# Spectral and shifted-MLP layer in fp16 halves: another order of low halves, GpSimd's refinement chains and the first shifted tiles

## The chip, the core and the metric

The kernel runs on one core of a Trainium2 chip. The core has five engines with instruction streams of their own: TensorE (PE in the profile; its weight loads are listed as PEld), VectorE (DVE), ScalarE (ACT), GpSimd (POOL) and SyncE (SP), which here issues DMAs. In this program they wait for each other through semaphores. The metric is the device time of one execution in microseconds (us), lower is better.

## The reference

Input x is 2048 rows of 448 features. It is normalised by row, and the normalised xn goes into two branches, whose results are added to x:

```python
xn = layernorm(x)
A  = irfft2(rfft2(xn) * (w_r + 1j*w_i))
h  = gelu(layernorm(xn) @ w1)                 # 448 -> 448
hs = concat(four quarters of 112 features of h,
            moved by +1, -1, +2, -2 rows, zeros let in) @ w2
x1 = xn + hs
B  = x1 + gelu(layernorm(x1) @ w3) @ w4       # 448 -> 1792 -> 448
out = x + A + B
```

All of it is fp32.

## The kernel before

Products are made in fp16 on TensorE: each operand is split into a high half (the value rounded to fp16) and a low half (what is left), and a product is the sum of high by high, high by low and low by high. So weights and activations are both split by other engines ahead of TensorE, usually the high half by ScalarE (a copy) and the low half by VectorE (scaled value minus high half).

The rows are cut into 16 blocks of 128: block b holds rows b, b + 16, b + 32 and so on, so that a shift by one row is a shift by one block. Blocks are worked in four groups of four: group 0 is blocks 14, 15, 0, 1, group 1 is 2 to 5, group 2 is 6 to 9, group 3 is 10 to 13. A block within a group is a unit (i from 0 to 3). What happens to a group, with the names in the code:

- `norm1` (from L322): mean and variance by VectorE (`sta` L309, `mva` L310), then a chain of tiny operations: `va` (L333, L334), a first guess of the inverse root in integers, `vy` (L335, L336), `nma` (L338). With it each block is normalised in place, one by each of the engines in the list `apply` (L345 for ScalarE, L348 for GpSimd and VectorE). The guess is coarse. GpSimd refines it meanwhile (L356 to L364), and makes from it the factor `gsc` (L365) that the gelu applies, and the scales of the later residual (`cs`, `nm`, L369 to L376).
- `turn_pe` (L396) transposes the group's four blocks on TensorE, by feature chunk t (0 to 3), 4 transposes each, into PSUM. `turn_copy` takes the high half out on ScalarE (L406) and the low half on VectorE (L407): xT. Group 3 is turned by DMA instead.
- `w1_in` (L446) does the product with w1, 44 matmuls for a group: 12 for each of chunks 0 to 2 and 8 for the short chunk 3. In group 0 all four units go forward together by chunk and by pass (high by high, high by low, low by high), as w1 is being split at the time; in later groups one unit at a time.
- `w1_unit` (L458): gelu on ScalarE (L466), high half (L467), low half on VectorE (L468), then a DMA transpose issued by SyncE (L471) puts the result, h, back with features on the partitions.
- `w2_tile` (L475): for one block, 12 matmuls (L487): three for each of the four quarters k. Quarter 2 is read from block b - 2, 0 from b - 1, 1 from b + 1, 3 from b + 2. So tile 0 needs blocks 14 and 15 (units 0 and 1 of group 0), 1 (unit 3) and 2 (unit 0 of group 1); tile 1 needs blocks 15 and 0, 2 and 3. VectorE adds the result to the block (L489).

After that come the second layernorm (`ln2`), the product with w3 (L417), gelu and halves `hf` (L732, L734, L735), the product with w4 (L754), in the function `front` and what calls it, and the two Fourier transforms as matrix products, woven in by halves c: among them `px` (L649), taken out of PSUM by ScalarE (`te`, L654) and multiplied by VectorE (L655, L656), added by GpSimd (L658).

`split_w` (L268 to L287) splits a weight tile. With `high=P` GpSimd scales it, makes the high half (L275) and the low one (L276); with `low=P` GpSimd scales (L279), ScalarE makes the high half (L281), GpSimd the low one (L282); without, ScalarE does the high half (L284), VectorE the low one (L285). `powers` finds a power of two for a tensor's scale, through one small matmul (`pm`, L254) that sums over partitions.

The order on each engine is fixed when the kernel is built: a scheduler simulates the program and issues each engine's instructions in the order in which they become ready there. `behind(key)` holds instructions back in that order until those recorded in `after[key]` have been issued; it adds no wait at run time. What runs at run time is therefore the order and the data's own semaphores. The program uses eight banks of PSUM, four names (`mm`, `tr`, `sp`, `acc`) of two each, which are handed on from user to user.

The main sequence (L825 to L895) begins with group 0, and goes on:

```python
    with behind("p2"):
        T1(1)
...
    with behind("a1"):
        w1_unit(0, 0, first[0])
        n1.append(norm1(2, [P, V, A, P], 1))
    with behind("a1"), behind("n", 2):
        for k in range(1, 4):
            w1_unit(0, k, first[k])
```

`first` are the four PSUM banks in which group 0's w1 product is summed up; `T1(g)` is `turn_pe` and `turn_copy` for all four chunks; `("n", 2)` is group 2's `nma`.

## Time and profile before

| | us |
|---|---|
| median of 3 runs | 415.0 |
| lowest, highest | 414.98, 415.24 |
| profiled execution, its time | 415.5 |
| its span, first to last instruction | 413.7 |
| TensorE busy within the span | 406.3 |
| VectorE, ScalarE, GpSimd busy | 297.8, 247.7, 113.4 |

The profile is of one execution; its span and its time differ by what lies ahead of the first instruction and behind the last. In a row of the timeline the first number is the start in us, the second the length; then come engine, source line, operation, output <- inputs by the program's names, shape, and how many instructions the row stands for. A bracket at the end gives idle time of that engine just before it and what ended it. Rows of matmuls are pipelined: a row's length includes about 0.16 us in which its last matmul drains while the next row has begun.

### The profile page before, as it was taken

The page shows a single profiled execution, that of the slowest core. Times are in us where ns is not written, and L with a number is a line of the kernel's source. Part 1 is how long each engine was busy: PE and PEld are TensorE (multiplying, and loading weights), DVE is VectorE, ACT ScalarE, POOL GpSimd, SP SyncE. Part 2 cuts the span into 40 slices and gives each one's busy share as a digit, 9 for nine tenths or more (in the row PEclk, how much of TensorE's full clock was granted, in tenths as well). Part 3 has the DMA queues.
Part 4 walks back from the last instruction along what each step waited for, and adds up shares of the span by engine and source line. Part 5 has one row for each costly group of instructions (what it writes and reads, how often), then busy time and mean ns, then how long its engine had stood idle before and what let it go on. Part 6 is the DMA issues. An engine that isn't in the chain of part 4 may idle for free.

```text
span 413.7 us, 8526 instructions
## 1 busy us (share of the span) xinstructions
PE 406.3 (98%) x3310; PEld 289.7 (70%) x3310; DVE 297.8 (72%) x636; ACT 247.7 (60%) x427; POOL 113.4 (27%) x204
## 2 busy tenths in 40 slices
PE   7998999999999999999999999999999999999996
PEld 3555555765667777776788888787766776677885
DVE  5998999798843757863688889865877687667122
ACT  4688869973647866762578888864443334342321
POOL 2697620101136746400031121210212221221000
PEclk9999999999999999999999999999999999999999
DMA  8959779914921374447056665620000113224001
GB/s 285 329 202 171 148 150 336 161 61 89 203 68 44 91 238 164 113 79 174 14 131 172 154 155 142 154 69 3 2 0 2 68 37 121 90 68 133 24 0 46
DMA packets 53496, 48.53 MB, mean 117 GB/s; under 512 B 37600, under 2 KB 48480, under 8 KB 53456
## 3 DMA queue, kind: packets, MB, share of 16 engines
q1 hardware_dynamic: 53456, 47.99, 43.7%
q8 instruction: 26, 0.43, 0.4%
q14 instruction: 14, 0.11, 0.1%
HBM read 35.52 MB, written 3.67 MB: 95 GB/s over the span
## 4 chain that ended last, share of the span: by engine, by line
PE 91%; POOL 3%; DVE 3%; DMA 2%; issue 0%; ACT 0%; POOLq 0%
PE pw L417 33%; PE acc L754 31%; PE pw L487 9%; PE pw L446 4%; PE pu L677 3%; PE ps L575 3%; PE pe L697 2%; PE pp L632 2%; PE px L649 2%; PE py L719 2%; DVE sta L309 1%; DMA xt<-x 1%; DMA h<-hs 1%; DVE xT L407 1%; POOL w2p L276 0%; POOL xt L348 0%
## 5 line engine op out<-in xcount | busy, mean ns | idle before, releaser
L417 PE MATMUL pw<-x2mem,w3p 128*128 128x256 f16 x1232 | 149.0, 273 | 0.0
L754 PE MATMUL acc<-w4p,hf 128*128 128x448 f16 (+1 forms) x714 | 138.1, 341 | 0.0
L417 PEld LDWEIGHTS <-w3p 128*128 128x128 f16 x1232 | 118.6, 98 | 19.1
L754 PEld LDWEIGHTS <-hf 128*128 128x128 f16 x714 | 69.4, 98 | 48.3 <-DVE hf L735 0.3
L732 ACT ACTIVATE pw<-pw,pe 128x512 f32<-128x512 f32 x56 | 36.7, 656 | 64.0 <-PE pw L417 64.0
L735 DVE SCALAR_TENSOR_TENSOR hf<-pw,h,hf 128x512 f16<-128x512 f32 x56 | 41.8, 748 | 40.9 <-ACT hf L734 40.6
L487 PE MATMUL pw<-w2p,h 112*128 112x448 f16 x192 | 40.0, 352 | 1.1 <-DMA h<-hs 1.1
L734 ACT ACTIVATE hf<-pw,h 128x512 f16<-128x512 f32 x56 | 38.1, 684 | 1.1
L658 POOL TENSOR_TENSOR z<-te 128x450 f32<-128x450 f32 x16 | 16.3, 1017 | 74.0 <-DVE te L656 74.0
L446 PE MATMUL pw<-w1p,xT 128*128 128x448 f16 x176 | 35.5, 352 | 0.4 <-ACT xT L406 0.3
L704 POOL TENSOR_TENSOR e<-e 128x226 f32<-128x226 f32 x16 | 11.3, 709 | 77.5 <-ACT e L701 74.7
L487 PEld LDWEIGHTS <-h 112*128 112x128 f16 x192 | 18.5, 98 | 17.3 <-DMA h<-hs 1.6
L446 PEld LDWEIGHTS <-xT 128*128 128x128 f16 x176 | 17.0, 98 | 16.5 <-ACT xT L406 0.9
L639 ACT ACTIVATE pf<-pp 64x450 f16<-64x450 f32 x32 | 17.3, 541 | 16.6 <-DVE pf L640 8.1
L701 ACT ACTIVATE e<-pe 128x452 f32<-128x452 f32 x16 | 8.8, 548 | 26.6 <-PE pe L697 26.6
L640 DVE TENSOR_TENSOR pf<-pp,pf 64x450 f16<-64x450 f32 x32 | 19.9, 621 | 5.3 <-ACT pf L639 5.0
L555 POOL TENSOR_TENSOR xr<-xf 128x452 f32<-128x452 f32 x8 | 9.2, 1155 | 31.6 <-issue 25.4
L654 ACT ACTIVATE te<-px 64x450 f32<-64x450 f32 x32 | 17.2, 539 | 0.5
L712 DVE TENSOR_TENSOR vh<-e,vh 128x448 f16<-128x448 f32 x16 | 10.0, 625 | 9.7 <-ACT vh L711 9.7
L566 DVE TENSOR_TENSOR xh<-f,xh 128x452 f16<-128x452 f32 x16 | 11.8, 780 | 6.9 <-ACT xh L565 6.9
L558 POOL TENSOR_TENSOR f<-xr 128x452 f32<-128x452 f32 x16 | 16.1, 1030 | 0.6
L706 DVE TENSOR_TENSOR e<-e 128x113 f32<-128x113 f32 x16 | 9.5, 593 | 7.8 <-POOL e L704 7.8
(171 smaller groups left out, 600.0 us busy)
## 6 DMA issues: line engine op xcount, KB each, us to landing
wc<-wf SPq DMA_DIRECT2D x32, 225.0 KB, 3.7
wl<-wf SPq DMA_DIRECT2D x8, 450.0 KB, 3.8
xf<-x SPq DMA_DIRECT2D x8, 448.0 KB, 3.5
xt<-x SPq DMA_DIRECT2D x3, 896.0 KB, 13.0
w3raw<-w SPq DMA_DIRECT2D x3, 896.0 KB, 16.0
xr<-x SPq DMA_DIRECT2D x12, 224.0 KB, 2.6
out<-xr SPq DMA_DIRECT2D x12, 224.0 KB, 2.0
gn<-c_g SPq DMA_DIRECT2D x16, 128.0 KB, 3.3
```

Source lines behind the costliest of these rows:

```text
L417: T.matmul(ps_out, wp[:, wi + t, cols], xT[:, xi + t, tok], start=t == 0 and wi + xi == 0, stop=t == 3 and wi == 4)
L446: m = T.matmul(pm[:, :D], xTs[g][:, xi + t, 128 * i:128 * i + 128], w1p[:, wi + t], start=t == 0 and p == 0, stop=t == 3 and p == 2)
L487: T.matmul(pm[:, :D], hT[g][:112, 4 * hi + k, o:o + 128], w2p[:, wi, k], start=n == 0, stop=n == 11)
L558: P.tensor_tensor(out=f[:, :, k:k + 2].rearrange("p b s d -> p s b d"), in0=u[:, :, 0], in1=u[:, :, 1], op=op)
L639: A.activation(out=hi, in_=src, func=AF.Copy)
L640: V.tensor_tensor(out=lo, in0=src, in1=hi, op=ALU.subtract)
L654: A.activation(out=e[64 * h:64 * h + 64], in_=px_[64 - 64 * h:128 - 64 * h, :2 * DF], func=AF.Copy)
L658: P.tensor_tensor(out=z, in0=t[:, 0], in1=t[:, 1], op=ALU.add)
L732: A.activation(out=pm, in_=pm, func=AF.Gelu_apprx_tanh, scale=r3)
L734: i = A.activation(out=h[:, 0], in_=pm, func=AF.Copy, scale=h3)
L735: j = V.scalar_tensor_tensor(out=h[:, 1], in0=pm, scalar=h3, in1=h[:, 0], op0=ALU.mult, op1=ALU.subtract)
L754: m = T.matmul(to, h[:, hi, o:o + 128], w4p[0][:, wi, f, r], start=f == 0 and n == 0, stop=f == 13 and n == 2)
```

## The change

In words, with the lines of the kernel before:

1. `split_w`: the splitting on GpSimd (`high=P`) now leaves the low half to be placed by the caller. A new form, used for chunk 1 of w1: GpSimd scales the tile into a spare buffer, ScalarE makes the high half, and GpSimd the low half. Before, VectorE made that low half (L285).
2. `norm1`: the factor `gsc` becomes a function of its own (`gain`), apart from the refinement and the scales. For group 2, `va` stands behind the halves of unit 3 of group 0 (`behind(0, 3)`), and its blocks are normalised by GpSimd, VectorE, ScalarE, VectorE instead of GpSimd, VectorE, ScalarE, GpSimd.
3. GpSimd's order: refinement and gain of group 0, then refinement and gain of group 1, then w2's scaling, high and low halves; the scales of groups 0 to 2 all stand behind w2's last low half.
4. `w1_unit`: in group 0 the gelu of unit i stands behind the halves of unit i - 2.
5. TensorE's order: group 1's first eight transposes and the small matmul of `powers` for w2 go ahead of the last four matmuls of group 0's w1 product, the other eight behind. That small matmul gets a bank of its own. `w2_tile` is cut in two for tiles 0 and 1: quarters 2 and 0 of both (12 matmuls), then group 2's transposes, then quarters 1 and 3 (12), then group 2's w1 product.
6. w2's quarters 1 and 3: scaled by GpSimd earlier, high half by ScalarE behind group 0's last halves, low half by GpSimd behind group 2's normalisation.
7. In the transform: `te` records its instructions, and the halves `hf` of front 4, unit 1, stand behind `te` of half 12 (one unit's halves, L734 and L735).

```diff
--- before.py
+++ after.py
@@ -272,9 +272,13 @@
             return i.ins, lambda: V.scalar_tensor_tensor(out=lo, in0=src, scalar=s, in1=hi, op0=ALU.mult, op1=ALU.subtract).ins
         if high is P:
             P.tensor_scalar(out=src, in0=src, scalar1=s, scalar2=0.0, op0=ALU.mult, op1=ALU.add)
-            P.tensor_scalar(out=hi, in0=src, scalar1=1.0, scalar2=0.0, op0=ALU.mult, op1=ALU.add)
-            i = P.tensor_tensor(out=lo, in0=src, in1=hi, op=ALU.subtract)
-            return (i.ins,)
+            i = P.tensor_scalar(out=hi, in0=src, scalar1=1.0, scalar2=0.0, op0=ALU.mult, op1=ALU.add)
+            return i.ins, lambda: P.tensor_tensor(out=lo, in0=src, in1=hi, op=ALU.subtract)
+        if isinstance(low, bass.AP):
+            P.tensor_scalar(out=low, in0=src, scalar1=s, scalar2=0.0, op0=ALU.mult, op1=ALU.add)
+            i = A.activation(out=hi, in_=src, func=AF.Copy, scale=s)
+            j = P.tensor_tensor(out=lo, in0=low, in1=hi, op=ALU.subtract)
+            return i.ins, j.ins
         if low is P:
             i = P.tensor_scalar(out=src, in0=src, scalar1=s, scalar2=0.0, op0=ALU.mult, op1=ALU.add)
             after["ws"] = (i.ins,)
@@ -330,8 +334,9 @@
         a = pc.tile([128, 2 * n], F32, name=f"va{b0}")
         yi = pc.tile([128, 2 * n], I32, name=f"vy{b0}")
         y = yi.bitcast(F32)
-        V.tensor_scalar(out=a[:, n:], in0=mv[:, :n, 1], scalar1=1.0 + EPS, scalar2=EPS * EPS, op0=ALU.mult, op1=ALU.add)
-        V.tensor_scalar(out=a[:, 0:n], in0=mv[:, :n, 1], scalar1=EPS, scalar2=None, op0=ALU.add)
+        with behind(0, 3) if g == 2 else contextlib.nullcontext():
+            V.tensor_scalar(out=a[:, n:], in0=mv[:, :n, 1], scalar1=1.0 + EPS, scalar2=EPS * EPS, op0=ALU.mult, op1=ALU.add)
+            V.tensor_scalar(out=a[:, 0:n], in0=mv[:, :n, 1], scalar1=EPS, scalar2=None, op0=ALU.add)
         V.tensor_single_scalar(yi, a.bitcast(I32), 1, op=ALU.logical_shift_right)
         V.tensor_scalar(out=yi, in0=yi, scalar1=-1, scalar2=0x5F3759DF, op0=ALU.mult, op1=ALU.add)
         nm = pc.tile([128, n], F32, name=f"nma{b0}")
@@ -362,7 +367,10 @@
             P.tensor_tensor(out=z, in0=z, in1=q, op=ALU.mult)
             P.tensor_scalar(out=z, in0=z, scalar1=-0.5 * 0.375 ** 3, scalar2=1.5 * 0.375, op0=ALU.mult, op1=ALU.add)
             P.tensor_tensor(out=r, in0=z, in1=w, op=ALU.mult)
-            P.tensor_scalar(out=gsc[:, 4 * g:4 * g + 4], in0=r[:, n:], scalar1=r1, scalar2=None, op0=ALU.mult)
+
+        def gain():
+            i = P.tensor_scalar(out=gsc[:, 4 * g:4 * g + 4], in0=r[:, n:], scalar1=r1, scalar2=None, op0=ALU.mult)
+            after["g", g] = (i.ins,)
 
         def scales():
             c, r1st, u = cs[:, 4 * g:4 * g + 4], w[:, 0:n], w[:, n:]
@@ -376,7 +384,7 @@
             P.tensor_scalar(out=nm1, in0=nm1, scalar1=-1.0, scalar2=None, op0=ALU.mult)
             for k, b in enumerate(bs):
                 xn_scale[b], xn_bias[b] = r1st[:, k:k + 1], nm1[:, k:k + 1]
-        return refine, scales
+        return refine, gain, scales
 
     after = {}
 
@@ -463,7 +471,8 @@
         pm = pm[:, :D]
         pv_ = pm.rearrange("p (k n) -> p k n", k=4)
         h = hs_buf[c % (HS if g == 3 else HS + 2)]
-        A.activation(out=pm, in_=pm, func=AF.Gelu_apprx_tanh, scale=gsc[:, c:c + 1])
+        with behind(0, i - 2) if g == 0 and i > 1 else contextlib.nullcontext():
+            A.activation(out=pm, in_=pm, func=AF.Gelu_apprx_tanh, scale=gsc[:, c:c + 1])
         u = A.activation(out=h[:, 0, :, 0:112], in_=pv_, func=AF.Copy, scale=h1)
         v = V.scalar_tensor_tensor(out=h[:, 1, :, 0:112], in0=pv_, scalar=h1, in1=h[:, 0, :, 0:112],
                                    op0=ALU.mult, op1=ALU.subtract)
@@ -472,10 +481,12 @@
         after[g, i] = u.ins, v.ins
         after["h", g, i] = (d.ins,)
 
-    def w2_tile(b):
-        pm = bank("sp", f"pw2_{b}")
-        n = 0
-        for k in (2, 0, 1, 3):
+    w2b = {}
+
+    def w2_mm(b, ks):
+        if b not in w2b:
+            w2b[b] = bank("sp", f"pw2_{b}")
+        for k in ks:
             src, o = b - SHIFT[k], 1
             if src < 0:
                 src, o = src + NB, 0
@@ -484,8 +495,13 @@
             g, i = WHERE[src]
             o += h_at(g, i) - 1
             for hi, wi in ((0, 0), (0, 1), (1, 0)):
-                T.matmul(pm[:, :D], hT[g][:112, 4 * hi + k, o:o + 128], w2p[:, wi, k], start=n == 0, stop=n == 11)
-                n += 1
+                m = T.matmul(w2b[b][:, :D], hT[g][:112, 4 * hi + k, o:o + 128], w2p[:, wi, k],
+                             start=k == 2 and hi + wi == 0, stop=k == 3 and hi == 1)
+        after["w2", b] = (m.ins,)
+
+    def w2_tile(b, ks=(2, 0, 1, 3)):
+        w2_mm(b, ks)
+        pm = w2b.pop(b)
         V.scalar_tensor_tensor(out=xb(b), in0=xb(b), scalar=cs[:, CS[b]:CS[b] + 1], in1=pm[:, :D],
                                op0=ALU.mult, op1=ALU.add)
 
@@ -651,8 +667,9 @@
         o = stage(f"te{c}", 6 * DF, c % 2)
         e, t = o[:, :2 * DF], o[:, 2 * DF:].rearrange("p (a n) -> p a n", a=2)
         for h in range(2):
-            A.activation(out=e[64 * h:64 * h + 64], in_=px_[64 - 64 * h:128 - 64 * h, :2 * DF], func=AF.Copy)
-        V.scalar_tensor_tensor(out=t[:, 0], in0=src, scalar=sc[:, 0:1], in1=w[:, 0], op0=ALU.mult, op1=ALU.mult)
+            i = A.activation(out=e[64 * h:64 * h + 64], in_=px_[64 - 64 * h:128 - 64 * h, :2 * DF], func=AF.Copy)
+        j = V.scalar_tensor_tensor(out=t[:, 0], in0=src, scalar=sc[:, 0:1], in1=w[:, 0], op0=ALU.mult, op1=ALU.mult)
+        after["te", c] = i.ins, j.ins
         V.scalar_tensor_tensor(out=t[:, 1], in0=e, scalar=sc[:, 2:3], in1=w[:, 1], op0=ALU.mult, op1=ALU.mult)
         z = pst.tile([128, 2 * DF], F32, tag="z", bufs=2, name=f"z{c}")
         P.tensor_tensor(out=z, in0=t[:, 0], in1=t[:, 1], op=ALU.add)
@@ -731,8 +748,9 @@
         with prio(EVAC):
             A.activation(out=pm, in_=pm, func=AF.Gelu_apprx_tanh, scale=r3)
             h = pw.tile([128, 2, 512], F16, tag="hf", bufs=3, name=f"hf{G}{fp}")
-            i = A.activation(out=h[:, 0], in_=pm, func=AF.Copy, scale=h3)
-            j = V.scalar_tensor_tensor(out=h[:, 1], in0=pm, scalar=h3, in1=h[:, 0], op0=ALU.mult, op1=ALU.subtract)
+            with behind("te", 12) if (G, fp) == (4, 1) else contextlib.nullcontext():
+                i = A.activation(out=h[:, 0], in_=pm, func=AF.Copy, scale=h3)
+                j = V.scalar_tensor_tensor(out=h[:, 1], in0=pm, scalar=h3, in1=h[:, 0], op0=ALU.mult, op1=ALU.subtract)
             after["f", G, fp] = i.ins, j.ins
         hs[G, fp] = h
 
@@ -837,66 +855,89 @@
         with behind("w1", t - 1):
             turn_copy(0, t, pts[t])
         with behind("a0", t):
-            after["w1", t] = split_w(w1p[:, t], w1p[:, 4 + t], w1s[:, t], s1, P if t > 1 else V) if t else (hi, low())
+            after["w1", t] = split_w(w1p[:, t], w1p[:, 4 + t], w1s[:, t], s1, P if t > 1 else xr[:, 0:D]) if t else (hi, low())
     h1 = pc.tile([128, 1], F32, name="h1")
     V.tensor_scalar(out=h1, in0=s1, scalar1=2.0 ** -5, scalar2=None, op0=ALU.mult)
-    for t in range(4):
+    for t in range(3):
         w1_in(0, list(enumerate(first)), [t], range(0 if t else 1, 3))
+    after["T", 1] = (w1_in(0, list(enumerate(first)), [3], [0]).ins,)
     with behind("ws"):
         n1[0][0]()
-    with behind("w1", 1):
+    with behind("a0", 1):
         n1.append(norm1(1, [P, V, A, V]))
     with behind("w1", 3):
         squares(m2[:112], flat(w2s[:112]))
     with behind("n", 1):
-        s2, r2 = powers(m2, 1, "2", first[0][:, 448:512], lambda: stats1(2, [0]))
+        pts = [turn_pe(1, t) for t in range(2)]
+        with behind("T", 1):
+            s2, r2 = powers(m2, 1, "2", "acc", lambda: stats1(2, [0]))
+        with behind("p2"):
+            after["T", 1] = (w1_in(0, list(enumerate(first)), [3], [2]).ins,)
     with behind("np", 1):
+        n1[0][1]()
+    with behind("g", 0):
         n1[1][0]()
-        for k in (2, 0):
-            after["w2p"] = split_w(w2p[:, 0, k], w2p[:, 1, k], w2s[:112, k], s2[:112], high=P)
-    with behind("p2"):
-        T1(1)
+        n1[1][1]()
+    pts += [turn_pe(1, 2), turn_pe(1, 3)]
+    for t in range(4):
+        turn_copy(1, t, pts[t])
+    with behind("g", 1):
+        for k in (1, 3):
+            P.tensor_scalar(out=w2s[:112, k], in0=w2s[:112, k], scalar1=s2[:112], scalar2=0.0, op0=ALU.mult, op1=ALU.add)
+        lows = [split_w(w2p[:, 0, k], w2p[:, 1, k], w2s[:112, k], s2[:112], high=P) for k in (2, 0)]
+    for hi, low in lows:
+        with behind("g", 1):
+            low()
     s12 = pc.tile([128, 4], F32, name="s12")
     V.tensor_tensor(out=s12[:, 0:1], in0=h1, in1=s2, op=ALU.mult)
     V.scalar_tensor_tensor(out=s12[:, 1:2], in0=r1, scalar=2.0 ** 5, in1=r2, op0=ALU.mult, op1=ALU.mult)
     V.tensor_scalar(out=s12[:, 2:3], in0=s12[:, 0:1], scalar1=s12[:, 0:1], scalar2=EPS, op0=ALU.mult, op1=ALU.mult)
     p12, eps12 = s12[:, 1:2], s12[:, 2:3]
+    stats1(2, [1])
     with behind("a1"):
-        w1_unit(0, 0, first[0])
-        n1.append(norm1(2, [P, V, A, P], 1))
-    with behind("a1"), behind("n", 2):
-        for k in range(1, 4):
+        for k in range(4):
             w1_unit(0, k, first[k])
-    with behind("na", 2):
-        for k in (1, 3):
-            split_w(w2p[:, 0, k], w2p[:, 1, k], w2s[:112, k], s2[:112], P)
+        n1.append(norm1(2, [P, V, A, V], 2))
+    for k in (1, 3):
+        with behind(0, 3):
+            A.activation(out=w2p[:, 0, k], in_=w2s[:112, k], func=AF.Copy)
+        with behind("np", 2):
+            i = P.tensor_tensor(out=w2p[:, 1, k], in0=w2s[:112, k], in1=w2p[:, 0, k], op=ALU.subtract)
+    after["w2p"] = (i.ins,)
     h_alloc(1)
     for k in range(4):
         w1_unit(1, k)
+    for b in range(2):
+        w2_mm(b, (2, 0))
+    after["T", 2] = after["w2", 1]
     T1(2)
     with behind("h", 1, 3):
         load_w3([3])
-    n1[2][0]()
-    with behind("np", 2):
-        n1[0][1]()
-    for n in n1[1:]:
-        n[1]()
+    with behind("w2p"):
+        n1[0][2]()
+        n1[1][2]()
+        for f in n1[2]:
+            f()
+    for b in range(2):
+        with behind("T", 2):
+            w2_tile(b, (1, 3))
     with behind("a2"):
         n1 = [norm1(3, [P, P, P, P])]
     h_alloc(2)
-    for k in range(4):
-        w1_unit(2, k)
+    with behind("w2", 1):
+        for k in range(4):
+            w1_unit(2, k)
     for k in range(4):
         with behind(*(("a2",), ("a2",), (2, 0), (2, 1))[k]):
             squares(m3[:, k:k + 1], w3raw[:, k])
     s3, r3 = powers(m3, 4, "3", "mm")
     h3 = pc.tile([128, 1], F32, name="h3")
     V.tensor_scalar(out=h3, in0=s3, scalar1=2.0 ** -5, scalar2=None, op0=ALU.mult)
-    for b in range(4):
+    for b in range(2, 4):
         w2_tile(b)
     turn(3)
-    n1[0][0]()
-    n1[0][1]()
+    for f in n1[0]:
+        f()
     ln2([0, 1], [A, P])
     with behind("t", 3), behind("h", 2, 3), behind("b0"):
         for i in range(4):
```

## The prediction

> **What bounds the kernel now.** I read the clock first, then the page's busy times and chain, then the list of what TensorE (PE) waited for, then the timelines around those waits.
>
> ```profile
> core 0: 413.7 us, clock 1.000
> PE 406.3 (98%) x3310; PEld 289.7 (70%) x3310; DVE 297.8 (72%) x636; ACT 247.7 (60%) x427; POOL 113.4 (27%) x204
> PE 91%; POOL 3%; DVE 3%; DMA 2%; issue 0%; ACT 0%; POOLq 0%
> PE pw L487 <- DMA h<-hs: 1.1, 1, 1.1
> PE pm L254 <- DVE pt L248: 0.9, 1, 0.9
> PE px L649 <- DVE te L655: 0.4, 1, 0.4
> PE pw L446 <- ACT xT L406: 0.3, 1, 0.3
> PE pw L254 <- DVE pt L248: 0.2, 1, 0.2
> ```
>
> PE works 406.3 of 413.7 us at full clock and holds 91% of the chain. The change keeps the number of PE's matmuls, so it can only remove or add PE's waits, and this list shows how few there are: behind the start-up only 1.1 us (the shifted product with w2, L487, on a DMA), 0.4 (L649), 0.3 and 0.2. Nothing larger than about 2 us is to be had. PE's timeline around the first two stages, and the transposes that the 1.1 waits for:
>
> ```profile
> 12.68 7.73 PE L446 MATMUL pw<-w1p,xT 128*128 128x448 f16 x40
> 20.57 0.38 PE L254 MATMUL pw<-pt,ones 128*128 128x1 f32 x2 [0.16 <-DVE pt L248]
> 20.82 1.94 PE L396 MATMUL pta<-ident,xt 128*128 128x128 f32 x16
> 22.86 8.71 PE L446 MATMUL pw<-w1p,xT 128*128 128x448 f16 x44
> 31.74 0.73 PE L487 MATMUL pw<-w2p,h 112*128 112x448 f16 x3
> 34.08 1.31 PE L487 MATMUL pw<-w2p,h 112*128 112x448 f16 x6 [1.06 <-DMA h<-hs]
> 47.36 2.81 PE L487 MATMUL pw<-w2p,h 112*128 112x448 f16 x14
> ...
> 27.23 1.34 SPq L471 DMA_TRANSPOSE h<-hs  x1
> 30.86 2.61 SPq L471 DMA_TRANSPOSE h<-hs  x2
> DMA to landing us min/median/max: 3.0/3.3/3.8
> ```
>
> The transpose of unit 0 of group 0 is issued at 27.23, that of unit 1 only at 30.86, and PE, at 34.08, starts just when it has landed (3.2 us later). Who made unit 1 late is on VectorE (DVE):
>
> ```profile
> 26.50 0.65 DVE L468 SCALAR_TENSOR_TENSOR hs<-pw,h,hs 128x448 f16<-128x448 f32 x1
> 27.58 0.88 DVE L335 TENSOR_SCALAR vy<-va 128x8 int32<-128x8 int32 x1
> 28.50 0.96 DVE L336 TENSOR_SCALAR vy<-vy 128x8 int32<-128x8 int32 x1
> 30.12 1.27 DVE L468 SCALAR_TENSOR_TENSOR hs<-pw,h,hs 128x448 f16<-128x448 f32 x2
> ```
>
> Between the low half of unit 0 and that of unit 1 stands group 2's normalising chain and its first normalised block: 3 us (27.1 to 30.12), 1.84 of them in two tiny operations.
>
> **Part 1: low halves first, gelus and high halves interleaved, w2's first tiles in two parts.** DVE now does the low halves of units 0 to 3 of group 0 in one run, 0.64 each (half of 1.27), and the chain behind them. ScalarE alternates gelu and high half, so a high half comes every 1.15 us or so; its first result isn't earlier. Starting from the same first low half (ends 27.15), the lows end near 27.2, 27.9, 28.6 and 29.4; SyncE's transposes stand 1.37 apart (2.61 less 1.24, the length of one), so they are issued near 27.2, 28.6, 29.9, 31.3, and land 3.2 later: 30.4, 31.8, 33.1, 34.5; group 1's first two follow near 36.0 and 37.4. Cutting tiles 0 and 1 puts the 12 matmuls that need only units 0 to 2 of group 0 first (0.189 each, from the L487 rows: 2.81 less 0.73, by 14 less 3 matmuls; 2.3 us), then group 2's 16 transposes (1.94), then the 12 that need unit 3 and group 1. With PE's first w2 matmul at 31.7, unit 2 is needed at about 33.4, unit 3 at 35.9, group 1's units at 36.5 and 37.7. So the 1.06 wait goes, with slacks of 0.3 (unit 2), 1.4, 0.5 and 0.3 behind it. Gain 1.06, bounds 0.5 (one transpose 0.5 late, the 3.8 of the landing row in place of 3.2) and 1.1. What is delayed in exchange is group 2's chain (va behind unit 3's low half, near 29.4): its normalised x is due for the transposes at about 34 and comes near 32. That costs nothing, by 2 us.
>
> **Part 2: GpSimd (POOL) takes w1's low half of tile 1 and runs group 0's refinement uncut ahead of group 1's share of the normalisation.** POOL's rows:
>
> ```profile
> 13.35 0.66 POOL L279 TENSOR_SCALAR w1s<-w1s,pe 128x448 f32<-128x448 f32 x1 [1.93 <-DMA w1s<-w]
> 13.97 0.20 POOL L356 TENSOR_TENSOR vq<-vy 128x8 f32<-128x8 f32 x1
> 14.25 0.20 POOL L357 TENSOR_TENSOR vq<-vq,va 128x8 f32<-128x8 f32 x1
> 15.93 1.04 POOL L282 TENSOR_TENSOR w1p<-w1s,w1p 128x448 f16<-128x448 f32 x1
> 17.34 1.03 POOL L282 TENSOR_TENSOR w1p<-w1s,w1p 128x448 f16<-128x448 f32 x1
> 19.27 0.94 POOL L348 TENSOR_SCALAR xt<-xt,vy,nma 128x448 f32<-128x448 f32 x1
> ...
> 12.82 0.68 DVE L285 SCALAR_TENSOR_TENSOR w1p<-w1s,pe,w1p 128x448 f16<-128x448 f32 x1
> ```
>
> Added on POOL: one scaling (0.66) in idle time before 13.35, and one subtraction (1.04, as the other low halves). Taken from DVE: 0.68. New order: after 13.97 one chain step, low halves of tiles 1, 2, 3 to about 15.2, 16.3, 17.7 (two steps between), then six chain steps 0.3 apart (13.97 to 14.25) to 19.4, then xt, 0.70 to 0.94, to 20.1 to 20.3. Tile 1's low half is needed by PE at 12.68 + 16 x 0.189 = 15.7, tile 2's at 18.0: slack 0.5 and 1.7. Group 1's transposes now stand before the last four matmuls of group 0, so PE reaches them at 19.48 and not at 20.24, and waits for xt: 0.8 idle in place of the old 0.33 before L254 (0.16 of it named), and 0.16 twice by the copies xT (the list's 0.3). These copies now have four matmuls more of cover. Net: +0.15; bounds -0.1 (xt at 20.1) and +0.8 (idle 1.4: xt at 20.9, where each of the six steps costs 0.1 more).
>
> Before, DVE's small chain (L333) was held behind such a POOL subtraction:
>
> ```profile
> 17.36 1.04 DVE L333 TENSOR_SCALAR va<-mva 128x4 f32<-128x4 f32 x1
> 18.31 0.15 DVE L334 TENSOR_SCALAR va<-mva 128x4 f32<-128x4 f32 x1
> 19.20 1.27 DVE L348 TENSOR_SCALAR xt<-xt,vy,nma 128x448 f32<-128x448 f32 x2
> 20.18 0.33 POOL L356 TENSOR_TENSOR vq<-vy 128x8 f32<-128x8 f32 x1
> ```
>
> L333 and its twin L334 do the same work; the first ended with POOL's L282 (17.34 to 18.37). This loss stays, as the chain again meets the last low half, but 0.6 earlier.
>
> The Trainium skill, "SBUF — State Buffer", section "Who interferes with whom", speaks against this part: VectorE and GpSimd share a port pair as an exclusive lock, and the one that comes second is blocked for the other's whole instruction. L333 agrees. In the other direction the trace does not: POOL's xt and L356 ran under DVE's two xt for 0.94 and 0.33 in place of 0.70 and 0.20. What the full lock would make of the time is rival 3.
>
> **Part 3: the scales' chains, w2's scaling and splits, another order of group 1's statistics.** These move POOL work after 20.3: refinement of group 1 (2.7 us), four scalings, two splits, to about 29.4. w2's low halves are then due at 31.7: slack 2.3, no cost; without that cover each would cost its 1.04. Zero, bounds 0 and 0.3.
>
> **Part 4: te of half 12 ahead of a gelu's halves (4,1).**
>
> ```profile
> 260.37 0.67 ACT L734 ACTIVATE hf<-pw,h 128x512 f16<-128x512 f32 x1
> 261.06 1.09 ACT L654 ACTIVATE te<-px 64x450 f32<-64x450 f32 x2
> 261.16 0.75 DVE L735 SCALAR_TENSOR_TENSOR hf<-pw,h,hf 128x512 f16<-128x512 f32 x1
> 262.19 0.69 DVE L655 SCALAR_TENSOR_TENSOR te<-px,sc,wc 128x450 f32<-128x450 f32 x1 [0.28 <-PE pu L677]
> 262.93 0.74 PE L649 MATMUL px<-pf,gn 128*128 128x225 f16 x6 [0.36 <-DVE te L655]
> ```
>
> PE's px waits for te's first product, which frees its bank. It moves ahead of hf's high half on ScalarE (0.67) and of hf's low half on DVE (0.75), thus by about 0.7, to end near 262.2. The wait, 0.36 by the row and 0.5 by the gap that precedes it in PE's starts, goes: gain 0.4, bounds 0.1 and 0.5. The halves hf come 1.1 later; their first reader, the product with w4, has 15 matmuls of L417 and more ahead of it. The lower bound is a new small wait there or at the next px.
>
> **Part 5: what of the early gain lasts.** A gain at 47 is kept only if the other engines follow. DVE does not have the room:
>
> ```profile
> 60.00:70.00 10.00, 10.00 (x55) 5.16 (x54) 10.00 (x14) 9.64 (x15) 0.00 (x0) 1.00 0.99 291
> 80.00:90.00 10.00, 10.00 (x71) 6.78 (x70) 10.00 (x29) 7.15 (x14) 0.00 (x0) 1.00 0.36 94
> ```
>
> The columns are PE, its weight loads, DVE, ScalarE, POOL. DVE is full for these 10 us each, but PE also shows no idle time (10.00), so there is some stock between them. DVE itself gains: 0.68 moved away, and 0.88 + 0.96 of blocked chain may shrink. I take 0.2 back, bounds 0 and 0.9 (all of it).
>
> **Sum.** -1.06 + 0.15 + 0 - 0.4 + 0.2 = -1.1; as three of the terms lean on slacks of 0.3 to 0.5, I take a further 0.2 for one of them missed: -0.9. The profiled execution took 415.5 with its span of 413.7, so 1.8 lie around it; the median of the three runs is 415.0, 0.5 below it. Span 412.8, profiled 414.6, median 414.1.
>
> **Rivals.**
> 1. The early gain is given back: PE arrives earlier at 55 to 110 and waits there for DVE, full at 10.00. For it: both rows of part 5. Against it: PE had no wait there. What stays is te: 415.0 - 0.4 = 414.6, or 414.9 with a new wait at the next px.
> 2. Nothing moves where it should: the transposes still wait (unit 2, 0.4 of slack), PE waits 0.8 at unit 2 or unit 3 and the 1.06 only changes its name. Against it: unit 1 moves by over 2 us. -0.3 + 0.15 - 0.4 + 0.2: 414.7.
> 3. The lock is whole: POOL's six chain steps after 17.7 stand out DVE's two xt (1.27, now from about 18.2). xt then ends at 21.5, PE idles 2.0 at 19.48 and the whole of part 1 shifts with it: -0.9 + 1.2 = 415.3. This is the Trainium skill's rule of part 2; the rows 0.94 and 0.33 give it little.
> 4. The other side, slower: POOL's uncut chain becomes PE's bound. Before, xt of group 1 was started at 19.27 with the chain cut around it; now each of six steps of 0.3, one behind the other, delays it. If three of them stretch as L335 and L336 did on DVE (0.88 and 0.96 where L334 took 0.15, so 0.7 more each: 2.1), xt ends at 22.3, PE idles 2.8: -0.9 + 2.1 = 416.2. It is slower than before from an xt later than 21.1 on, measurably from 22.0. Against it: the chain steps in the rows above took 0.20 to 0.33.
>
> **How the numbers follow.** Forecast 0.58, rival 1 0.10, rival 2 0.10, rival 3 0.07, rival 4 0.15. What a measurement of this kernel can tell from no change is 0.2%, 0.83 us: faster means below 414.17, slower above 415.83. The forecast lies close to this edge: its own range is 413.3 to 414.6, of which I give 0.44 to faster and 0.14 to same, since the terms that I rounded (the 0.2 for a missed slack, the 0.2 of part 5) were both taken against the change. Rivals 1 and 2 lie within the bound with 0.15 and reach below it with 0.05, where te's gain is at its upper end; rival 3 is same, rival 4 slower. Faster 0.49, same 0.36, slower 0.15. Lowest: all terms at their favourable bounds, 415.0 - 1.1 - 0.1 - 0.5 = 413.3. Above, rivals 1 to 3 are taken in (415.3) with 0.3 for part 3's bound, 415.6; rival 4 is left out. Range 413.3 to 415.6.
>
> **What would show it.** Part 1: no wait of L487 on a transpose near 34, low halves back to back on DVE, w1 of group 2 done near 46.5. Part 2: PE idle 0.6 to 1.0 before the transposes at 20.3; over 2 is rival 3 or 4. Part 4: px at 262 without a wait. Part 5: waits between 55 and 110 that the old list hasn't. Wrong would be a new wait over 1 us in PE's list, or part 1's 1.06 still there.

## The result and the profile after

| | before | after |
|---|---|---|
| median, 7 runs each | 415.0 us | 413.64 us |
| lowest, highest | 414.68, 415.24 | 413.39, 414.05 |
| ratio of times, 95% interval | | 0.9968, 0.9956 to 0.9979 |
| profiled execution: its time, its span | 415.5, 413.7 | 413.43, 411.7 |

The change made the kernel faster by 1.36 us, 0.3%, and the interval lies below 1. The forecast was 414.1, 0.9 faster. First the list of what TensorE waited for in the changed kernel:

```profile
PE wps L808 <- DVE wsrc L186: 1.2, 1, 1.2
PE pw L454 <- ACT xT L414: 0.3, 1, 0.3
PE px L665 <- DVE te L671: 0.2, 1, 0.2
```

The line numbers are those of the changed kernel (L454 was L446, L665 was L649, L498 is the w2 product that was L487, L480 the DMA transpose, L477 the low half); in some of the runs below they stand one or two lines further on. The wait of 1.1 us on the DMA transposes of h is gone, and TensorE does not wait before group 1's transposes at 19.47 either. TensorE's timeline there:

```profile
12.66 6.97 PE L454 MATMUL pw<-w1p,xT 128*128 128x448 f16 x36
19.47 1.05 PE L404 MATMUL pta<-ident,xt 128*128 128x128 f32 x8
20.36 0.28 PE L254 MATMUL pm<-pt,ones 128*128 128x1 f32 x2
20.50 0.92 PE L454 MATMUL pw<-w1p,xT 128*128 128x448 f16 x4
21.25 1.04 PE L404 MATMUL pta<-ident,xt 128*128 128x128 f32 x8
22.13 8.65 PE L454 MATMUL pw<-w1p,xT 128*128 128x448 f16 x44
30.62 2.44 PE L498 MATMUL pw<-w2p,h 112*128 112x448 f16 x12
32.89 1.91 PE L404 MATMUL pta<-ident,xt 128*128 128x128 f32 x16
34.64 2.47 PE L498 MATMUL pw<-w2p,h 112*128 112x448 f16 x12
36.95 8.49 PE L454 MATMUL pw<-w1p,xT 128*128 128x448 f16 x44
45.28 6.98 PE L498 MATMUL pw<-w2p,h 112*128 112x448 f16 x36
```

Read it by the starts: group 2's w1 product ends at 45.28, against 47.36 before. All of the gain is there: it is 2.08 us, and the spans differ by 2.0. But the two profiles do not begin alike, and a part of the 2.08 belongs to the first profile's execution. GpSimd's timeline in the changed kernel shows it, beside the row of 13.35 in the prediction:

```profile
11.38 1.61 POOL L283 TENSOR_SCALAR w1s<-w1s,pe 128x448 f32<-128x448 f32 x2
18.42 0.95 POOL L353 TENSOR_SCALAR xt<-xt,vy,nma 128x448 f32<-128x448 f32 x1
```

In the changed kernel's execution the last part of w1 had landed by the time that GpSimd wanted it (11.4 us by the trace, 13.2 before), though its load is issued at the same place in the same queue. GpSimd's part of group 1's normalisation therefore started at 18.42 and not at the 19.4 of the prediction. That raised the first question for the runs: did the change bring the load earlier, or was it this execution?

### The profile page after: what moved, and what is told of

It is laid out like the page before. It is cut to its first block, busy times and chain, and to the rows that moved or that the text cites. A ratio compares the mean times of both kernels' runs of the same rounds, so it can differ in the third digit from the quotient of the medians.

```text
span 411.7 us, 8524 instructions
## 1 busy us (share of the span) xinstructions
PE 406.6 (99%) x3310; PEld 290.2 (70%) x3310; DVE 295.9 (72%) x636; ACT 247.4 (60%) x427; POOL 115.1 (28%) x205
## 4 chain that ended last, share of the span: by engine, by line
PE 91%; ACT 4%; DVE 3%; issue 1%; POOL 0%; DVEq 0%; POOLq 0%
PE pw L425 30%; PE acc L772 29%; PE pw L498 9%; PE pw L454 8%; PE ps L591 3%; PE pe L714 2%; PE py L736 2%; PE wps L808 2%; PE pp L648 2%; ACT te L670 2%; PE pu L694 1%; PE px L665 1%; PE pta L404 1%; DVE te L673 1%; ACT zb L682 1%
## 5 line engine op out<-in xcount | busy, mean ns | idle before, releaser
L425 PE MATMUL pw<-x2mem,w3p 128*128 128x256 f16 x1232 | 149.0, 272 | 0.0
L772 PE MATMUL acc<-w4p,hf 128*128 128x448 f16 (+1 forms) x714 | 138.3, 341 | 0.0
L425 PEld LDWEIGHTS <-w3p 128*128 128x128 f16 x1232 | 118.6, 98 | 18.8
L772 PEld LDWEIGHTS <-hf 128*128 128x128 f16 x714 | 69.4, 98 | 48.2 <-DVE hf L753 0.4
L498 PE MATMUL pw<-w2p,h 112*128 112x448 f16 x192 | 39.1, 352 | 0.0
L454 PE MATMUL pw<-w1p,xT 128*128 128x448 f16 x176 | 35.1, 352 | 0.3 <-ACT xT L414 0.3
L498 PEld LDWEIGHTS <-h 112*128 112x128 f16 x192 | 18.6, 98 | 16.4 <-DMA h<-x2mem 0.3
L454 PEld LDWEIGHTS <-xT 128*128 128x128 f16 x176 | 17.1, 99 | 16.0 <-ACT xT L414 0.5
```

What stands on the lines that cost most here:

```text
L425: T.matmul(ps_out, wp[:, wi + t, cols], xT[:, xi + t, tok], start=t == 0 and wi + xi == 0, stop=t == 3 and wi == 4)
L454: m = T.matmul(pm[:, :D], xTs[g][:, xi + t, 128 * i:128 * i + 128], w1p[:, wi + t], start=t == 0 and p == 0, stop=t == 3 and p == 2)
L498: m = T.matmul(w2b[b][:, :D], hT[g][:112, 4 * hi + k, o:o + 128], w2p[:, wi, k], start=k == 2 and hi + wi == 0, stop=k == 3 and hi == 1)
L772: m = T.matmul(to, h[:, hi, o:o + 128], w4p[0][:, wi, f, r], start=f == 0 and n == 0, stop=f == 13 and n == 2)
```

## The experiments

A method used below: for each matmul I took the time to the next one's start, less what its columns take at the full rate seen elsewhere (0.189 us for 448 columns). Summed up, and compared at the same amount of work done, this shows where one execution gains on another. These gaps by the starts are somewhat longer than the idle times in the brackets.

Each ratio is to the kernel before, timed in the same set of runs: its median was 414.94 us for experiments 1 and 2, 414.99 for 3 to 6, on another chip, and 414.82 for 7 to 9. The changed kernel was timed in the first of these sets alone, so "above the changed kernel" means above that set's 413.65. Of the kernels made by an edit of the changed kernel, only that of experiment 4 has an interval clear of the changed kernel's 0.9954 to 0.9978; for the others, what a part is worth is read from the traces.

**1. Both kernels again.** No edit. What is profiled here is called the second execution of each.

> The changed kernel itself, a second profiled execution. Theory A (the loads' landing differs from one execution to the next): the last part of w1 lands anywhere between the 11.4 us of the first profile of it and the 13.2 us of the kernel before; if it lands near 13, PE idles up to 0.8 us before group 1's transposes and the span is 0.5 to 0.9 above 411.7. Rival B (the change itself brings the loads earlier): 11.4 again, no PE wait at 19.5, span 411.5 to 412.0. Ratio to before 0.996 to 0.997 by both.

> The kernel before itself, a second profiled execution. Theory A: the last part of w1 lands somewhere else than at 13.16 us, and the span follows it little (TensorE's waits before group 1 stay at 0.3 + 0.16 + 0.16 or shrink): 413.2 to 413.8. Rival B: it lands at 13.2 again. Ratio 1.000, within 0.001.

The changed kernel: 413.65 us median, ratio 0.9966 (0.9954 to 0.9978), span 411.7. The kernel before: 414.94, ratio 1.0004 (0.9994 to 1.0014), span 413.1. The last part of w1 landed at 12.2 in the changed kernel and at 11.6 in the kernel before, so it is the execution and not the change that moves it. In the eleven profiles of this document in which that load was not moved by an edit, it landed at 11.4 to 12.2 in eight and at 12.9 to 13.2 in three. The waits of the second execution of the kernel before:

```profile
...
PE pm L254 <- DVE pt L248: 1.0, 1, 1.0
PE pw L487 <- DMA h<-hs: 0.9, 1, 0.9
PE px L649 <- DVE te L655: 0.4, 1, 0.4
PE pw L446 <- ACT xT L406: 0.3, 1, 0.3
```

The 0.2 on L254 near 20 has gone, and the 1.1 is 0.9. At equal work the prediction's own profile ends up 0.57 us behind this one, 0.43 more at the wait near 20 and 0.2 more at that on the transposes, less 0.13 at the start, and its time of 415.5 stood 0.5 above the median. That the late load made these waits is likely; no run separates it. Put side by side, the two second executions differ by 1.45, which fits the medians (1.29) better than the first pair:

| where | us |
|---|---|
| start, up to 12 us (when w1's first parts landed) | -0.18 |
| group 1's transposes and w1 product (12 to 31) | -0.32 |
| w2's first tiles (31 to 40) | -0.91 |
| 40 to 250, no row over 0.2 | -0.15 |
| px of half 13, near 260 | -0.27 |
| px of half 15, near 269 | +0.38 |
| rest | 0.00 |

**2. The te part, taken away from the changed kernel and put alone on the kernel before.**

```diff
-            with behind("te", 12) if (G, fp) == (4, 1) else contextlib.nullcontext():
+            with contextlib.nullcontext():
```

> The change without its last part (hf of front 4 no longer behind te of half 12). My reading: the part gained 0.27 us at px of half 13 and lost 0.39 at px of half 15 in the profile, so this kernel is within 0.2 us of the changed one, rather faster by 0.1: ratio 0.9965. Prediction's part 4: slower than the changed kernel by 0.4 us, ratio 0.9977.

> Only the last part of the change, on the kernel before. My reading: the wait of 0.36 us at px of half 13 shrinks to about 0.2 and one of about 0.2 to 0.4 appears at px of half 15: ratio 1.000. Prediction's part 4: 0.4 us faster, ratio 0.999.

Without it: 413.47 us, ratio 0.9963 (0.9950 to 0.9976), 0.18 below the changed kernel in the same set of runs, and the spans 411.6 and 411.7. Alone on the kernel before: 415.14, ratio 1.0006 (0.9996 to 1.0017). The part gains nothing. TensorE with it and, below, without it:

```profile
260.23 0.74 PE L665 MATMUL px<-pf,gn 128*128 128x225 f16 x6
...
269.59 0.74 PE L665 MATMUL px<-pf,gn 128*128 128x225 f16 x6 [0.21 <-DVE te L671]
```

```profile
260.79 0.74 PE L665 MATMUL px<-pf,gn 128*128 128x225 f16 x6 [0.35 <-DVE te L671]
...
270.37 0.74 PE L665 MATMUL px<-pf,gn 128*128 128x225 f16 x6
```

The named wait moved from half 13 to half 15. By the spacing of the matmuls the part takes the gap at the first from 0.52 to 0.25 and that at the second from 0 to 0.38. The `te` product that half 15's px waits for is no later for it: it ends at 269.54 with the part and at 269.57 without. What differs is TensorE's order, which the scheduler made anew: three matmuls of L425 and three of L772, 0.9 us together, stand ahead of that px without the part and behind it with the part. So TensorE comes there earlier and waits. The same two gaps, 0.26 and 0.38, stand in the profile of the part alone. The pair of intervals overlaps, so that this part costs 0.1 to 0.2 is likely and not settled; that it doesn't gain 0.4 is.

**3. Late loads.** In the changed kernel half of w2 is loaded ahead of group 1's x and of w1's last part.

```diff
+    SY.dma_start(w2s[:112, 0:2], w2[:, 0:2])
     load_x(1)
     SY.dma_start(w1s[64:128, 3], w1[384:448])
-    SY.dma_start(w2s[:112], w2)
+    SY.dma_start(w2s[:112, 2:4], w2[:, 2:4])
```

> The changed kernel with half of w2 loaded ahead of group 1's x and of the last part of w1, so that both land about 1.6 us later (near 13 to 13.6 in place of 11.4 to 12.2), as late as in the first profile of the kernel before. Theory A (GpSimd's queue behind that load is what sets group 1's transposes): its xt ends near 20.5, TensorE idles 0.6 to 1.2 us at 19.5, as the prediction had it, and the span is 0.6 to 1.2 above 411.7 (ratio 0.998 to 0.9995). Rival B (enough slack stands between GpSimd and TensorE): no wait at 19.5, span within 0.3 of 411.7.

414.46 us, ratio 0.9985 (0.9975 to 0.9995). The part landed at 13.6. From GpSimd's and TensorE's timelines:

```profile
13.65 0.64 POOL L284 TENSOR_SCALAR w1s<-w1s,pe 128x448 f32<-128x448 f32 x1 [0.93 <-DMA w1s<-w]
19.66 0.70 POOL L354 TENSOR_SCALAR xt<-xt,vy,nma 128x448 f32<-128x448 f32 x1
```

```profile
13.38 6.97 PE L455 MATMUL pw<-w1p,xT 128*128 128x448 f16 x36
20.42 1.09 PE L405 MATMUL pta<-ident,xt 128*128 128x128 f32 x8
```

GpSimd's xt starts at 19.66 and ends at 20.36, close to what the prediction said for a load at 13.2; TensorE goes on at 20.42. It idled only 0.23 there, because this execution was 0.74 late already from w1's first parts (13.38 against 12.63 in the changed kernel's second execution). Had TensorE come at the usual 19.47, the same xt would have made the 0.9 of idle time; no execution shows that. So the prediction's arithmetic of GpSimd's queue holds, under the load that it took from the old profile; in the changed kernel's own two executions the load is earlier and the wait does not exist. At equal work this execution stands 1.05 behind the second one of the changed kernel: 0.74 from the start, 0.25 from this wait. A start as late, by 1.0, stands in experiment 5 too, where no load was moved. The medians differ by 0.8; how much of that is the wait is open.

**4. Group 2's chain ahead of the low halves again.** In the changed kernel.

```diff
-        with behind(0, 3) if g == 2 else contextlib.nullcontext():
+        with contextlib.nullcontext():
...
-        with behind(0, i - 2) if g == 0 and i > 1 else contextlib.nullcontext():
+        with contextlib.nullcontext():
...
-        for k in range(4):
-            w1_unit(0, k, first[k])
+        w1_unit(0, 0, first[0])
         n1.append(norm1(2, [P, V, A, V], 2))
+    with behind("a1"), behind("n", 2):
+        for k in range(1, 4):
+            w1_unit(0, k, first[k])
```

> The changed kernel with group 2's normalising chain ahead of the low halves of units 1 to 3 again, and four gelus before the high halves, as before the change. Theory A (the order on VectorE made the old wait for the transposes): unit 1's low half comes about 2 us later, TensorE idles 0.7 to 2.5 us near 31, span 0.7 to 2 above 411.7. Rival B (cutting the first tiles in two is what removed the wait): idle under 0.3.

417.6 us, ratio 1.0058 (1.0046 to 1.0070): 4 us above the changed kernel, and slower than the kernel before. VectorE and TensorE, each from its own timeline:

```profile
25.70 0.67 DVE L477 SCALAR_TENSOR_TENSOR hs<-pw,h,hs 128x448 f16<-128x448 f32 x1
26.30 0.97 DVE L340 TENSOR_SCALAR vy<-va 128x8 int32<-128x8 int32 x1
27.30 0.95 DVE L341 TENSOR_SCALAR vy<-vy 128x8 int32<-128x8 int32 x1
29.67 1.26 DVE L477 SCALAR_TENSOR_TENSOR hs<-pw,h,hs 128x448 f16<-128x448 f32 x2
```

```profile
31.07 0.73 PE L498 MATMUL pw<-w2p,h 112*128 112x448 f16 x3 [0.30 <-DVE hs L477]
33.61 2.98 PE L498 MATMUL pw<-w2p,h 112*128 112x448 f16 x9 [1.81 <-DMA h<-hs]
36.38 2.53 PE L404 MATMUL pta<-ident,xt 128*128 128x128 f32 x16
```

Unit 1's low half comes 3.3 us behind the end of unit 0's, with two tiny operations blocked for 0.97 and 0.95. TensorE waits 1.81, more than the old 1.06, as the new order asks for unit 1 three matmuls after the start and has no transposes to put ahead. And something that no theory had: the nine matmuls behind the wait take 2.98 us where twelve of them took 2.44 in the changed kernel (row 30.62). The last section returns to it. The order of the low halves is thus a condition of cutting the tiles, not only a gain beside it.

**5. The first two tiles whole.** In the changed kernel, behind group 2's transposes.

```diff
-    for b in range(2):
-        w2_mm(b, (2, 0))
-    after["T", 2] = after["w2", 1]
     T1(2)
...
-            w2_tile(b, (1, 3))
+            w2_tile(b)
```

> The changed kernel with w2's first two tiles uncut, behind group 2's 16 transposes. Theory A (the cut gives the chain of group 2 and the transposes of h the time they need): the transposes wait at 30.6 for VectorE's normalised x, ready near 31.4, so 0.7, and unit 0 of group 1 lands at 35.2, where it is needed at 34.9: 0.3 more; span 0.5 to 1.2 above 411.7. Rival B (the low halves' order is all): within 0.2 of 411.7.

414.2 us, ratio 0.9984 (0.9974 to 0.9994): 0.55 above the changed kernel by the medians. The transposes wait, for VectorE's block:

```profile
31.60 0.56 PE L404 MATMUL pta<-ident,xt 128*128 128x128 f32 x3
32.42 1.64 PE L404 MATMUL pta<-ident,xt 128*128 128x128 f32 x13 [0.26 <-DVE xt L353]
```

The gap is 0.48 by the starts; the second wait that I expected, for unit 0 of group 1, isn't there. This execution's start was 1.0 later than usual, so its span of 413.1 overstates the loss. At equal work, and without the start, it falls back by 0.54 at the transposes and gets 0.13 back near 35: 0.4 in all.

**6. Chunk 1's low half on VectorE again.** In the changed kernel.

```diff
-... split_w(..., P if t > 1 else xr[:, 0:D]) if t else (hi, low())
+... split_w(..., P if t > 1 else V) if t else (hi, low())
```

> The changed kernel with the low half of w1's chunk 1 on VectorE again (0.68 us) and off GpSimd (0.8 and 1.03). Theory A: VectorE's chain for group 1 starts 0.6 later, its two normalised blocks end at 19.4 to 19.9 in place of 18.8, TensorE waits 0 to 0.4 for them: span 0 to 0.4 above 411.7. Rival B (GpSimd is what stands last before the transposes): GpSimd's xt comes earlier and the span falls by up to 0.2.

414.08 us, ratio 0.9977 (0.9967 to 0.9986), 0.43 above the changed kernel, but not for theory A's reason:

```profile
12.70 3.19 PE L454 MATMUL pw<-w1p,xT 128*128 128x448 f16 x16
16.07 3.94 PE L454 MATMUL pw<-w1p,xT 128*128 128x448 f16 x20 [0.17 <-DVE w1p L289]
19.84 1.04 PE L404 MATMUL pta<-ident,xt 128*128 128x128 f32 x8
```

TensorE waits at 15.7, by 0.34, for the low half itself: on VectorE it now stands behind group 1's four statistics (13.21 to 15.40), which the change puts first. At 19.84 there is no wait. Moving the half to GpSimd is what allows the statistics to go ahead.

**7. The order of part 1 alone, on the kernel before.** `behind(0, 3)` for va, the gelus in turn, and norm1 behind the four units, as in the change; the tiles are left to the scheduler.

```diff
-        w1_unit(0, 0, first[0])
-        n1.append(norm1(2, [P, V, A, P], 1))
-    with behind("a1"), behind("n", 2):
-        for k in range(1, 4):
-            w1_unit(0, k, first[k])
+        for k in range(4):
+            w1_unit(0, k, first[k])
+        n1.append(norm1(2, [P, V, A, P], 1))
```

> The kernel before with the order of part 1 alone: gelus and high halves of group 0 in turn, the four low halves ahead of group 2's chain (its tiles of w2 are then placed by the scheduler, which puts six matmuls of tiles 0 and 1 each ahead of the transposes). Theory A (the low halves' order made the wait for the transposes of h): no wait of L487-489 on a transpose near 33, span 0.6 to 1.1 below the 413.1 of the second look at the kernel before, ratio 0.9975 to 0.9985. Rival B (GpSimd's new order is needed too, as w2's last low halves come behind group 2's chain): TensorE waits there for GpSimd, gain under 0.4, ratio above 0.999.

414.48 us, ratio 0.9999 (0.9987 to 1.0012), short of theory A's 0.9975 to 0.9985; the median is 0.34 below that of the kernel before in the same runs (414.82), and the interval doesn't tell it from none. By the trace the wait of 0.85 to 1.06 becomes one of 0.27:

```profile
33.67 1.91 PE L397 MATMUL pta<-ident,xt 128*128 128x128 f32 x16
35.42 0.73 PE L489 MATMUL pw<-w2p,h 112*128 112x448 f16 x3
36.43 0.93 PE L489 MATMUL pw<-w2p,h 112*128 112x448 f16 x4 [0.27 <-DMA h<-x2mem]
```

The scheduler puts twelve matmuls ahead of the sixteen transposes here, as the cut tiles do (the twelve start at 31.27). At equal work this execution gains 0.46 on the second one of the kernel before at the tiles, of the 0.91 of the whole change. TensorE now waits for unit 0 of group 1, fifth in SyncE's queue, not for GpSimd as rival B had it. This says what else the change does: its queue of transposes starts earlier. The first issue is at 25.84 in the second execution of the changed kernel, 26.96 here:

```profile
25.84 4.10 SPq L480 DMA_TRANSPOSE h<-hs  x3
```

```profile
26.96 4.10 SPq L473 DMA_TRANSPOSE h<-hs  x3
```

The five are 1.36 to 1.46 apart in both, so every later one keeps the 1.1 us. In the changed kernel VectorE's first low half starts at 25.11, here at 26.21: the copies xT end earlier, as half of group 1's transposes come before four matmuls, and two of group 2's statistics in place of three stand ahead of it (1.16 us, 1.68).

**8. Group 1's transposes all behind group 0's product.** In the changed kernel.

```diff
-    for t in range(3):
+    for t in range(4):
         w1_in(0, list(enumerate(first)), [t], range(0 if t else 1, 3))
-    after["T", 1] = (w1_in(0, list(enumerate(first)), [3], [0]).ins,)
...
-        pts = [turn_pe(1, t) for t in range(2)]
-        with behind("T", 1):
-            s2, r2 = powers(m2, 1, "2", "acc", lambda: stats1(2, [0]))
-        with behind("p2"):
-            after["T", 1] = (w1_in(0, list(enumerate(first)), [3], [2]).ins,)
+        s2, r2 = powers(m2, 1, "2", "acc", lambda: stats1(2, [0]))
+    with behind("p2"):
+        pts = [turn_pe(1, t) for t in range(2)]
```

> The changed kernel with all of group 1's transposes behind the last four matmuls of group 0 again. Theory A (those four matmuls cover the copies xT, as part 2 of the prediction had it): a wait of 0.16 each comes back at the fourth chunk's transposes or at the first w1 matmuls of group 1, 0.1 to 0.3 in all: ratio 0.9970 to 0.9973. Rival B: no difference, 0.9966.

413.97 us, ratio 0.9980 (0.9971 to 0.9989), 0.32 above. By the starts the trace has a gap of 0.26 ahead of group 1's first w1 matmul, two of 0.03 behind it and one of 0.15 at 24.7; the changed kernel has the last of these alone. Between 22 and 31 us this kernel falls back by 0.32 in all, and the kernel before has the same four gaps there. That is theory A's mechanism, with a loss just above its 0.3; the ratio lies above its 0.9973.

**9. Two attempts at a faster one.** The changed kernel without the te part and with w1's last part loaded ahead of group 1's x; and the same with GpSimd's xt of group 1 ahead of group 0's refinement.

```diff
+    SY.dma_start(w1s[64:128, 3], w1[384:448])
     load_x(1)
-    SY.dma_start(w1s[64:128, 3], w1[384:448])
```

```diff
-    with behind("ws"):
-        n1[0][0]()
     with behind("a0", 1):
         n1.append(norm1(1, [P, V, A, V]))
+    with behind("np", 1):
+        n1[0][0]()
```

> The changed kernel without its te part and with the last part of w1 loaded ahead of group 1's x. Theory A (in executions with late loads GpSimd waits for that part, and TensorE for GpSimd): the lower half of the runs as without the te part, 413.4, the upper half lower; median 413.2 to 413.5. Rival B: group 1's x now lands later and sets VectorE's chain: up to 0.5 slower, 413.9.

> The same, and GpSimd's share of group 1's normalisation ahead of group 0's refinement chain. Theory A (in undisturbed executions neither sets TensorE's time): 413.2 to 413.5, the same as without this. Rival B (the gelus of group 0 then wait for the factor gsc, ready near 21.7 against 22.9 when the first gelu starts): slower by 0.2 or more if the chain ends later than 22.9.

The first: 413.5 us, ratio 0.9970 (0.9959 to 0.9981), no different from the kernel without the te part. The second: 414.01, 0.9978 (0.9970 to 0.9987), worse. Its gelus were not late (first at 23.07, gsc done at 22.18), so rival B's reason falls; TensorE has a new wait:

```profile
34.99 1.93 PE L498 MATMUL pw<-w2p,h 112*128 112x448 f16 x9
37.11 0.74 PE L498 MATMUL pw<-w2p,h 112*128 112x448 f16 x3 [0.18 <-DMA h<-hs]
```

VectorE's timeline has the reason:

```profile
28.88 0.90 DVE L340 TENSOR_SCALAR vy<-va 128x8 int32<-128x8 int32 x1
29.82 0.96 DVE L341 TENSOR_SCALAR vy<-vy 128x8 int32<-128x8 int32 x1
```

With xt first, GpSimd's chains end later, and its two low halves of w2 run from 28.72 to 30.75 (26.21 to 28.24 in the changed kernel), across group 2's `vy`, which took 0.17 each there. The low half of unit 1 of group 1 comes later for that, its transpose is issued at 33.80 in place of 32.78, and TensorE waits for it, by 0.35. So group 0's refinement "uncut and ahead of xt" keeps w2's low halves clear of group 2's chain. None of these beats the kernel without the te part, 413.47.

## Why the prediction came out as it did

The direction and the place were right: the gain is in TensorE's waits before 40 us, and nothing of the gain there was given back by 250 us. The sum of -0.9 was nearer to the result than its terms deserved: part 2 came out 0.47 lower than written down and part 4 some 0.5 higher, and these two errors cancel. The 0.2 of part 5 and the 0.2 for a missed slack were not needed either.

- **Part 1, -1.06.** Right in mechanism, shown by experiments 4 and 5 and by the trace of 7. Like for like it is -0.91, as the old 1.06 held 0.2 that the second execution doesn't have. The slacks of 0.3, 1.4, 0.5 and 0.3 came out as 0.3 to 0.4, 1.3, none and 0.1 to 0.2, but by luck, as both sides of them moved. The prediction kept the first low half where it was ("ends 27.15"), but it ended near 25.8, and the queue of transposes with it moved by 1.1 to 1.4 us; and TensorE began with w2 at 30.62 in place of the 31.7. With the queue of experiment 7 a wait of 0.27 was left. What is left in the changed kernel is one of 0.12 near 35 in the second execution and 0.02 in the first.
- **Part 2, +0.15.** This step failed in size and in sign: it measured -0.32. TensorE's idle time of 0.8 before group 1's transposes did not occur, since w1's last part lands at 11.4 to 12.2 in most executions and the working used 13.2, from the one profile there was. With a load at 13.6 the xt of the prediction came where it said (experiment 3). The old 0.33 that it replaces is not in the kernel before's second execution either. What remains is the gain from the copies' cover, and it is the whole of the -0.32 (experiment 8). Its size was right by luck: the prediction called it "the list's 0.3", but that 0.3 is one wait in group 0, near 11.0, and the changed kernel's list still has it; the gaps that went are those of experiment 8. VectorE's blocked va, 1.04 in the first profile, was 0.17 in the second execution of the kernel before, so that "this loss stays" was an accident of timing too.
- **Part 3, 0.** No wait for w2's halves appeared. The prediction saw no gain in the order of statistics; by the traces of experiment 7, one less of group 2's ahead of the first low half is part of what brought that earlier.
- **Part 4, -0.4.** This step failed: +0.1 net, -0.27 and +0.38. The prediction allowed for a new wait at the next px only as far as it left a gain of 0.1; it is larger than the gain. It came two halves on, where the scheduler's new order brings TensorE earlier to a te that is where it was (experiment 2).
- **Part 5, +0.2.** Measured 0: the 1.41 gained by 47 is still 1.46 at 101 and 1.56 at 250, though VectorE is busy 10.00 in 60 to 70 and 80 to 90 in the changed kernel's second execution too:

```profile
60.00:70.00 10.00, 10.00 (x58) 5.43 (x56) 10.00 (x17) 8.96 (x16) 1.44 (x1) 1.00 0.95 339
80.00:90.00 10.00, 10.00 (x68) 6.43 (x67) 10.00 (x28) 7.29 (x11) 1.10 (x1) 1.00 0.13 53
```

VectorE, though full, was far enough ahead of TensorE; a busy share of 10.00 was not by itself a bound. Rival 1 falls with it, and rival 2 with the wait of 1.1.

Rivals 3 and 4 fall as well: GpSimd's chain steps took 0.20 to 0.26 but for one of 0.45 under VectorE's two xt, and its xt 0.95. Each of these two began when some 0.4 of an xt of VectorE (0.51) was left, and took 0.25 longer. So rival 3's 1.2 was too much. The Trainium skill ("SBUF — State Buffer", section "Who interferes with whom") has the engine that comes second blocked for the other's whole instruction. The prediction read 0.94 and 0.33 as speaking against that; with so little of VectorE's instruction left, the rows here neither show it nor exclude it. In the other direction it is what experiment 4 shows, 0.97 and 0.95 for operations of 0.17, each ending with one of GpSimd's two low halves of w2 (26.20 to 28.23).

## What to carry to other kernels

One profile is one execution: before a wait goes into a sum, ask whether the load that ends it lands at the same time in another execution. An order of small operations is worth as much as the queue behind it: the first low half 1.1 us earlier moved five transposes that follow each other at a nearly fixed spacing, and the same cut of the tiles with the old order cost 4 us. Where a scheduler makes the order, holding back one unit's work (the te part) can change the order on other engines too; here the wait moved two steps on with it, so look for the next reader before counting the gain.

## What the runs showed of the hardware

The landing of loads varied with nothing changed in their queue: w1's last part landed at 13.2 and 11.6 in two executions of the kernel before, at 11.4 and 12.2 in two of the changed one. TensorE's start moved too, by up to 1.0 us between executions at full clock (experiment 5).

TensorE's granted clock fell to half, for 3.41 us, shortly after an idle time of about 2 us, in two profiled executions. In the kernel with the te part alone the profiled execution had w1's third part late (8.6 against 7.7), and TensorE waited 2.14 us between its warm-up and the first small matmul. Windows and timeline of that execution (the number behind POOL's is the granted clock):

```profile
10.00:20.00 10.00, 9.70 (x50) 6.15 (x51) 8.91 (x28) 6.83 (x12) 6.82 (x16) 0.83 1.01 317
```

```profile
10.30 0.38 PE L254 MATMUL pm<-pt,ones 128*128 128x1 f32 x2 [2.14 <-DVE pt L248]
12.05 1.67 PE L446 MATMUL pw<-w1p,xT 128*128 128x448 f16 x4
```

The clock was 0.50 from 10.85 to 14.26 and 1.00 around it. The four matmuls took 1.67 us, against 0.92 for four of the same shape in the changed kernel's 20.50 row. In experiment 4 the wait of 1.81, shortly after one of 0.30, was followed by 0.83 too, 0.50 from 34.23 to 37.64:

```profile
30.00:40.00 10.00, 7.89 (x40) 4.67 (x38) 5.96 (x10) 5.62 (x11) 7.86 (x36) 0.83 0.88 161
```

There the nine matmuls lost 1.1 us (2.98 against nine at 0.189 and the drain) and the sixteen transposes 0.6 (2.53 against 1.91), so some 1.7 of this execution's 4 us are this clock and the rest the waits. Five of that kernel's six executions list a mean clock of 0.996; the sixth lists 0.999, took 416.99, and wasn't profiled, so its 3.3 above the changed kernel are not explained. Waits of 0.9 to 1.4 us in the other executions left it at 1.00 or 0.999. The Trainium skill, "TensorE: Matmul & The Clock Gate", Part 1, gives an idle window of about 3.4 us, free-running, before the clock is halved; the 3.41 us at half clock agree with its length, but as idle time 2.14 us, and 0.30 and 1.81 with three matmuls between, were enough here. The profiled execution of the te part alone took 416.49 us against its median of 415.14, with a mean clock of 0.995. Of five times above 416 among the runs of the kernel before, four list 0.995 or 0.996 as well and one, 416.21, lists 0.999; none of those was profiled.
